# Five inversion rounds instead of six, and seven products in four more groups of an MLP

## The chip, the cores and the metric

The kernel runs on one core of one Trainium2 chip. The metric is the device time of one execution in microseconds; the median of three runs before the change is 639.98 us.

## The reference

Attention with a delta rule for 4 batches, 8 heads, 768 tokens and a head width of 48, then a Fourier mixing over tokens and features, a layer norm and an MLP 384 to 1536 to 384, all in fp32:

```python
k_n = k / (np.linalg.norm(k, axis=-1, keepdims=True) + 1e-06)
state = np.zeros((B, H, D, D), dtype=np.float32)
for t in range(S):
    kt, vt, bt = (k_n[:, :, t], v[:, :, t], beta[:, :, t, None])
    y[:, :, t] = np.einsum('bhd,bhde->bhe', q[:, :, t], state)
    v_old = np.einsum('bhde,bhd->bhe', state, kt)
    state = state + bt[:, :, :, None] * np.einsum('bhd,bhe->bhde', kt, vt - v_old)
...
x = np.ascontiguousarray(y.transpose(0, 2, 1, 3)).reshape(B, S, H * D)
mixed = np.real(np.fft.fft(np.fft.fft(x, axis=1), axis=2)).astype(np.float32)
u = x + mixed
mu = np.mean(u, axis=-1, keepdims=True)
var = np.mean((u - mu) ** 2, axis=-1, keepdims=True)
un = (u - mu) / np.sqrt(var + 1e-06)
ch = np.maximum(un @ w_ch1, 0.0) @ w_ch2
return (u + ch).astype(np.float32)
```

## The kernel before

**Units and rounds.** A unit is 128 tokens of one batch with its eight heads; there are 24 of them, `u` = 0 to 23, six to a batch (batch 1 is units 0 to 5, in the code `b = 0`). In a unit the recurrence over tokens becomes the inverse of a unit lower triangular matrix for each head, put together from blocks of 32 by 32. A round takes several units through one inversion (`begin`, `invert`): the blocks stand in one tile `rr` of 128 x 1024, 30 steps of a product (L878) and a sum (L883) on VectorE, two scale multiplies (L677, L892) and two transposes by blocks (L662, L895). The tile always has place for four units. Batch 1 goes by a way of its own in two rounds; batches 2 to 4 go in the six rounds that `SIZES` tells. After its inversion a unit's chain (`ahead`, `step`, `outputs`) carries the state on and writes its rows of `x`.

**Slots.** A unit's data (`k`, `q`, `v` and what is made of them) lie in a slot; there are six, and unit `u` takes `slots[u % GS]`. `R1` is the mixing buffer: the folds (L1257 to L1263) write it and the sequence transform (`seq6`) reads it and writes the input of the feature transform (`feat`) into it.

**Mixing and MLP.** When a batch's six units are done, `mixing(b)` folds `x` over tokens and features, does the two transforms by matmuls with tables, normalises, and gives the MLP three groups of 256 tokens. A group's MLP has six chunks of 256 hidden values. `mlp` is the plain form: `first(i)` is 6 matmuls of 256 columns into one PSUM bank, its ReLU is copied to `R0`, and `second(i)` is 4 matmuls of 384 columns, accumulated over the six chunks in two banks. `mlpw` has the second layer in seven products, 7 matmuls of 192 columns a chunk in four banks: for these VectorE makes difference tables of the weights (`tables`, L1572), four sums of the hidden values a chunk (`sums`, L1642), and combines the products at the end (L1779). In this chip's fp32 one matmul of the program is two passes of TensorE. `mlpw` is used for the last group of batch 3 and all three of batch 4.

**Order.** Every engine issues in the order of the program. `Plan.op` only lists operations; `Plan.issue` reads the string `ORDER`, which names the operation, where there is a choice its engine, and the PSUM banks it takes, and sometimes a filler matmul (L2056 to L2062, behind them no one waits). So the string sets the order on all engines.

Of the kernel before, what the change touches and what calls it, by code (L numbers as in the profile page):

```python
# [16 lines left out]
SIZES = 3, 3, 3, 3, 3, 3  # L17
# [17 lines left out]
WF = 2, 2  # L35
NW, IV, IV1, WP = 9, 7.4111, 10.4756, -12.4024
# [29 lines left out]
IeIkErCwuADGBGeCOAOAJhEsGBFNBJFJFFLJDE5CF2JHJHHFCFOHHKBEuBF5CJKJKEzFCE6BHGCGaBFRCJEFSCE2FPCDOGfBFQCJ
TJTEtCFTEJiJSJSE3CJjF3JUJUE7DrBFUCHLHE8CE9BNnE7F6GFXCGgNzFSDsBFWCE+F7CJRJRJkFVCDhDhGhF+CJlE-BJLNoNoH
NGiFeHMJNFfEBFgBF8CIuFYHFFhCGjGlCF9BFiFaCJMFbCGF4CFZBJVJOF-FFcBDDFjCGmHGCCNqNqJmFnNsNsGnCFdBJPwuAJXG
DBN-FzFkGABFoCNrE6HOFpCDxDxJWFqFmCJQGBCFrCGEGFHPJnJnIUGoCGKFlCJYGGCOCOCDgGFCGHCFOQOQGNCJZGpBHSGJoJoG
MCGqBDtCKBKBGLBEHTBJrJrwuAIWJpJpGkBGOIXJqJqHVBGrHGJCJsJsGPBHUCGICGsCGTHRCJaOPGsGQHWCNtNtGUCGVBN3N3Gv  # L70
CImGWGtCNpNpHQBGRCInKCKCGuCHXGGXBGSCNuNuG2ORORGwCHIvG4CG5BN4N4HYCG3FBJtOSOSHZBHbBOBOBGyCG6IoJvJ0J0Gz
EHGxBNwNwG7CDuBJ+J+G1CG-G0BJzJzG8HACHBBOgOgHaCJuN8N8HCDpG+CJ1J1OTCGG9BNvGZIwJ2J2HcHEOUCKsRYRYHDCKrHe
CHiOVCJwHfCEKvHkCJxHdCHjGFHlBHhCHgCKtHoOfHjKzJ9J9HmKuRvKvODHBKyHnCKwRbRbHqCHpBIfHrKAKAOECOFBJ-J-HtCH
sBRcRcK0HuRkRkK1OGECN0N0HvCK4NxNxJ3HzRXRXK7KxHwHBN6N6OJH1CRwRwK8OWDFHyCHxBK2NyNyH0BK3RjRjH2OaOZRgRgK
DK-LNAGRaRaK6OIK5H4CRsRsJ5KEK9RoRoLCOHLDKFK+RZRZLWBELARxRxH3CLBOXLGOYN7FiLEOLJyRyRyOKObLOLFRnLWLKLIR
fHsLJLHR-K5LLLXSASALMKMKMIYOhOhLPONN1N1IgOiOiOeN9N9LYJ4LUCLTCSCSCOMJ6RpRpLQBN+N+RzHDJ7LcCLZBKOKOwvGO
cLaCLbCR1BLfCGLVCSfJ8LoBFLgOdLeCKYKYLhLSCLiLxDGSBSBOOLpLjKWKWLRCR0COjCFKLKLLqLyLrN5N5LkwuAOlCKXKXLsR
2HGOkCRmRmLdBLlKGSQSQLmLtOmBFKHKJKJR6LuL0SPOILvLnL6AELwKVKVOrMYOoLzOnMVMZCOpL7MWDOtMaCMDEBKIMXCOqKjK
jOuMmCMEN2N2OwRdRdKfKfReReKKKKL1OyMbDKkKkOzO5KZL2SRSRMGRqRqKbL8O0SSSSO1R7L9R4RlRlMFL3O6KhKhO2MpBKNKN
RiRiMcBKgKgRhRhR5R8KiKiKaMgAKcMqBKdO3KPO+O-KRPAMHMfEDR3O7CKQPBShPCPDOsPEPFL4PGMnCL+MdGKlPHPIPJPKKSPL  # L80
R9PMSDBHKeMeCSTFCL-KTSECMjGSFBKnMISVCPNSUCPOKmR+PPSGBHKUSWCFSKSJPQMiPRSaMhCPSMASXSLSISOSHSYSNSbSdMBP
TMkCSeKoMlSgKpL5MCSiMzMMABPUPVMoPWMNSjPXMwMOKqPYMPM0GPZMrM1CPaPbPcPdPeSkPfMxBSlPgMsMyCPhPiMQSmM2AMJP
jMKPkPlSnMRPmSuPnM4GPoM3CSvPpPqScMuSwMSSxPrM6BAPsM5CSySpPtPuSzS0PvO4PwPxS1M9PySqS2SsCPzP0SZP1P2S3P3S
4SrCP4M7FP5P6O8CP7M+DM8CSMQZQaS5O9BNASoS6P8P9S7Q4S8P+GS9QbCP-CS+M-CQAHMLS-NBFQCCTAMTQBCTBTCTDTETFMtN
DTGNCCTHQcCQDCTIQECMUTJTKTLQFGDTMQdETNYVYVQGFCQgCTOYUTKNEHTPQICQHBQJCTQQLCQhCTRTSTTTUNGTVNFCTWQKCQ5Q
fCTXQeCTYTZTaQMCQ6GQNQiFHTbQODETcQoCYYNBNLNHQnCTdRrLuQmCNOQQCTeTfQ7BTgThQPTiQjCHNJQSFTjQlCQUGEQkCQTY
JTgQ8ATkQRCNIYfQSQpHCQ-CTlYgYgQVCNPFTmRACQqYKYKQ9BNMDRtRtTnNQCQ+BQtBToQrCRBCFTpQsCQWYLYLNNCQuRCAHYhY
hRHCTqQvGDQXCYMYMRECNRBYiYiQxCQwRuRuRFCTrRDCYXYXQYc1YjHDULZOQzCUMYlCQ1AEYkCQ0UNDTsYwYwQyCYmCHYOYOUOC
RGBQ3YvQxRIGDTtNSBUPFRLCTuEYqYoNTBTvBYNTuURCRKBUSCYnUQBStBUTCYyYyRJYtYsUqRMEYpYQYQTwGYxYxRNUUFDTxCYr
# [159 lines left out]
def kernel(  # L249
# [24 lines left out]
    GS = 6  # L274
# [1821 lines left out]
```

## Time and profile before

| | |
|---|---|
| runs | 639.98 us median of 3 (639.46 to 642.2) |
| profiled execution | 640.02 us, of which the span is 638.2 us |
| TensorE clock granted | 0.999 |
| PE matmul / weight load busy | 616.2 us (97%) / 509.8 us (80%) |
| DVE (VectorE) busy | 522.3 us (82%), 1563 instructions |
| ACT (ScalarE) busy | 268.2 us (42%) |
| POOL (GpSimd) busy | 30.4 us (5%) |
| HBM | 25.82 MB read, 4.72 MB written |

In the profile a line such as "L351 PE MATMUL pp<-w,R 128*128 128x384 f32 x384 | 133.3, 491 | 0.0" is a group: source line, engine, operation, output and inputs, the part of the array that is used, the shape, the count, then busy us, mean ns of one, and idle time ahead of them. L351 is the helper through which nearly all matmuls go. Matmuls overlap, so their spacing is read from starts. `R` is `R0` or `R1`, `w` the MLP's weights or memory beside them, `gd`, `rr`, `tmp` the inversion's tiles, `eo` and `pm` the mixing's, `us` slots.

### The profile page before, as it was taken

The page shows a single profiled execution, that of the slowest core. Times are in us where ns is not written, and L with a number is a line of the kernel's source. Part 1 is how long each engine was busy: PE and PEld are TensorE (multiplying, and loading weights), DVE is VectorE, ACT ScalarE, POOL GpSimd, SP SyncE. Part 2 cuts the span into 40 slices and gives each one's busy share as a digit, 9 for nine tenths or more (in the row PEclk, how much of TensorE's full clock was granted, in tenths as well). Part 3 has the DMA queues.
Part 4 walks back from the last instruction along what each step waited for, and adds up shares of the span by engine and source line. Part 5 has one row for each costly group of instructions (what it writes and reads, how often), then busy time and mean ns, then how long its engine had stood idle before and what let it go on. Part 6 is the DMA issues. An engine that isn't in the chain of part 4 may idle for free.

```text
span 638.2 us, 22753 instructions
## 1 busy us (share of the span) xinstructions
PE 616.2 (97%) x9694; PEld 509.8 (80%) x9694; DVE 522.3 (82%) x1563; ACT 268.2 (42%) x837; POOL 30.4 (5%) x42
## 2 busy tenths in 40 slices
PE   8988989999999999999999999999999999999997
PEld 7667889876778777877777778778778789999997
DVE  5998899899998788999876899998846868767554
ACT  6898856442454426415754323433322112322120
POOL 2022411010000000000000000000000000000000
PEclk9999999999999999999999999999999999999999
DMA  8747454400022342100231430000000000010002
GB/s 206 223 122 164 109 117 91 115 2 1 1 40 52 74 90 60 20 2 2 41 71 38 88 80 1 2 25 4 2 4 3 1 2 1 2 50 2 26 1 74
DMA packets 87171, 32.01 MB, mean 50 GB/s; under 512 B 77724, under 2 KB 82557, under 8 KB 87069
## 3 DMA queue, kind: packets, MB, share of 16 engines
q1 hardware_dynamic: 86877, 30.32, 20.1%
q8 instruction: 76, 1.25, 0.8%
q14 instruction: 26, 0.21, 0.1%
q10 hardware_dynamic: 192, 0.23, 0.1%
HBM read 25.82 MB, written 4.72 MB: 48 GB/s over the span
## 4 chain that ended last, share of the span: by engine, by line
PE 76%; DVE 11%; SPq 3%; DMA 3%; ACT 3%; issue 2%; DVEq 0%; ACTq 0%
PE pp L351 73%; SPq L402 3%; PE pp L354 2%; DMA x<-in_moe_w_ch_dram 2%; DVE R L1257 1%; ACT us L360 1%; DMA us<-in_q_dram 1%; DVE tmp L768 1%; DVE w L774 1%; DVE w L1850 1%; PE pp L2056 1%; DVE eo L1257 1%; DVE tmp L878 1%; DMA ws<-in_moe_w_ch_dram 1%; DVE rr L797 0%
## 5 line engine op out<-in xcount | busy, mean ns | idle before, releaser
L351 PE MATMUL pp<-R,w 128*128 128x256 f32 (+1 forms) x832 | 180.8, 366 | 0.0
L351 PEld LDWEIGHTS pp<-R,w 128*128 128x128 f32 x832 | 146.1, 190 | 19.2
L351 PE MATMUL pp<-w,R 128*128 128x384 f32 x384 | 133.3, 491 | 0.0
L351 PEld LDWEIGHTS pp<-w,R 128*128 128x128 f32 x384 | 70.6, 190 | 41.1 <-issue 0.3
L360 ACT ACTIVATE us<-pp 128x256 f32<-128x256 f32 (+3 forms) x205 | 67.2, 342 | 76.1 <-PE pp L351 54.2
L351 PE MATMUL pp<-us 64*64 64x64 f32 (+4 forms) x2784 | 72.8, 230 | 3.1 <-issue 1.7
L351 PEld LDWEIGHTS pp<-us 64*64 64x64 f32 (+2 forms) x2784 | 60.1, 131 | 11.8 <-issue 6.0
L878 DVE TENSOR_TENSOR tmp<-rr 128x108 f32<-128x108 f32 (+11 forms) x180 | 59.6, 336 | 2.8
L883 DVE TENSOR_TENSOR rr<-rr,tmp 128x108 f32<-128x108 f32 (+11 forms) x180 | 57.7, 326 | 2.6
L1511 ACT ACTIVATE R<-pp 128x512 f32<-128x512 f32 x37 | 21.9, 593 | 69.4 <-PE pp L351 69.4
L351 PE MATMUL pp<-u,us 64*64 64x48 f32 (+2 forms) x1472 | 44.2, 216 | 4.0 <-issue 2.1
L351 PEld LDWEIGHTS pp<-u,us 64*64 64x64 f32 (+1 forms) x1472 | 38.0, 130 | 10.5 <-issue 4.9
L1686 DVE TENSOR_TENSOR us<-us,pp 128x256 f32<-128x256 f32 x64 | 26.4, 415 | 18.4 <-ACT us L360 14.5
L360 ACT ACTIVATE us<-us,nr 128x48 f32<-128x48 f32 x120 | 28.5, 322 | 9.0 <-DVE nr L685 8.4
L360 ACT ACTIVATE R<-pp 128x384 f32<-128x384 f32 (+7 forms) x50 | 19.2, 403 | 29.8 <-PE pp L354 16.1
L351 PE MATMUL pp<-st,us 48*64 48x48 f32 (+1 forms) x1232 | 28.8, 222 | 2.1 <-issue 1.1
L351 PEld LDWEIGHTS pp<-st,us 48*64 48x64 f32 x1232 | 23.8, 134 | 8.3 <-issue 5.5
L360 ACT ACTIVATE u<-pp 64x192 f32<-64x192 f32 (+1 forms) x54 | 17.6, 325 | 28.5 <-PE pp L351 27.5
L360 ACT ACTIVATE x<-pp 64x192 f32<-64x192 f32 (+1 forms) x60 | 19.5, 324 | 20.1 <-PE pp L351 17.5
L2062 PE MATMUL pp<-pack 64*64 64x256 f32 (+1 forms) x186 | 27.6, 384 | 0.0
L351 PE MATMUL pp<-us,gd 128*128 128x192 f32 x144 | 27.5, 326 | 0.0
L351 PEld LDWEIGHTS pp<-ft,R 97*128 97x128 f32 (+1 forms) x192 | 23.8, 191 | 2.8 <-ACT R L360 0.3
(185 smaller groups left out, 994.5 us busy)
## 6 DMA issues: line engine op xcount, KB each, us to landing
out_dram<-x SPq DMA_DIRECT2D x11, 384.0 KB
x<-in_moe_w_ch_dram SPq DMA_DIRECT2D x11, 242.0 KB
R<-in_moe_w_ch_dram SPq DMA_DIRECT2D x8, 256.0 KB
us<-in_k_dram SPq DMA_DIRECT2D x36, 48.0 KB
us<-in_q_dram SPq DMA_DIRECT2D x36, 48.0 KB
us<-in_v_dram SPq DMA_DIRECT2D x36, 48.0 KB
ws<-in_moe_w_ch_dram SPq DMA_DIRECT2D x5, 242.0 KB
us<-in_k_dram SPq DMA_DIRECT2D x6, 192.0 KB
```

The source lines that it names most:

```text
L351: I(nc.tensor.matmul(o, lhsT=lhsT, rhs=rhs, start=start, stop=stop, skip_group_check=True))
L354: I(nc.tensor.matmul(o, lhsT=src, rhs=ident[p0:p0 + n, p0:p0 + n], is_transpose=True, start=start, stop=True, skip_group_check=True))
L360: I(nc.scalar.activation(o, i, ACT.Copy, **({} if scale is None else {"scale": scale})))
L402: I((nc.sync if q == "SP" else nc.scalar).dma_start(out=o[x], in_=i[x]))
L768: I(eng(e).tensor_tensor(T_, sub(j + 1, 16, j, j + 1).broadcast_to([128, 2, n, j]), sub(j, j + 1, 0, j).broadcast_to([128, 2, n, j]), op=A ...
L774: I(eng(e).tensor_tensor(w, w, T_, op=ALU.add))
L878: I(eng(e).tensor_tensor(T_, R[:, :, j + 1:32, j:j + 1].broadcast_to([128, ns, n, j]), R[:, :, j:j + 1, 0:j].broadcast_to([128, ns, n, j]) ...
L883: I(eng(e).tensor_tensor(R[:, :, j + 1:32, 0:j], R[:, :, j + 1:32, 0:j], T_, op=ALU.add))
L1257: I(eng(e).tensor_tensor(o, i0, i1, op=op))
L1511: I(nc.scalar.activation(o, s, ACT.Relu))
L1686: vec(256, lambda e: I(nc.vector.tensor_tensor(o, i0(), i1(), op=ALU.add)), [], [aH] + list(wr), pr - P.ev, use=n)
L2062: I(nc.tensor.matmul(pst[bank][x, 0:256], lhsT=w[x, 0:128 // tiles], rhs=w[x, 0:256], start=True, stop=True, skip_group_check=True))
```

## The change

Constants, with the order string replaced as a whole:

```diff
-SIZES = 3, 3, 3, 3, 3, 3
+SIZES = 4, 4, 4, 3, 3
+PLACE = (0, 1, 2, 3, 4, 5, 0, 1, 2, 3, 6, 7, 4, 5, 0, 1, 2, 3, 4, 5, 0, 1, 2, 3)
+SPARE = 10, 11
...
+BEFORE = (1, 0), (1, 1), (2, 0), (2, 1)
...
 ORDER = """
-APBABAaAbAbAZwrAAAAcAcACDAKBA-A-AIBAYAEBBABAA9A9A+A+AQDAODAGDAFDALDAdBCAJDAUDARAfCANDAeCAgEFAHDICICA
+APBAAAQDAbAbAGBANBATyMAAHBABAcAcACBAaAFBAMBA9A9ALBADBAKBA-A-AEDAZAODA+A+AYBABAAIDAJDAdBCARAgDEAeCAfB
```

Two slots more in the mixing buffer, for units 10 and 11; what reads or writes them is ordered with the rest of that buffer (`z.own`):

```diff
+    slots += [(R1, SLOT), (R1, 0)]
...
-        z.t, z.o = slots[u % GS]
+        z.extra = u in SPARE
+        z.t, z.o = slots[PLACE[u]]
+        z.key = (id(z.t), z.o) if z.extra else id(z.t)
```

The scale multiplies of `begin` and `invert` become two, of 512 and 256 columns, that leave out a part above the diagonal:

```diff
-        vec(1024, lambda e: I(nc.vector.tensor_tensor(
-            R, R, gb[:, 32:64][:, :, None].broadcast_to([128, 32, 32]), op=ALU.mult)),
-            [agb(1)], [aR], pr, port=True)
+        for x, y in ((slice(16, 32), 32), (slice(0, 16), 16)):
+            vec(16 * y, lambda e, x=x, y=y: I(nc.vector.tensor_tensor(
+                R[:, x, 0:y], R[:, x, 0:y], gb[:, 32:64][:, x, None].broadcast_to([128, 16, y]), op=ALU.mult)),
+                [agb(1)], [A(rr0, o + 32 * x.start, o + 32 * x.stop)], pr, port=True)
```

The first two groups of batches 2 and 3 (`BEFORE`) go through `mlpw`, with a plain first layer, their tables in the mixing buffer (built anew for each of the two batches behind its feature transforms), the sums in `ws`, the hidden values in `R0` in a ring of two, and three PSUM banks: product 4 is split into 128 and 64 columns in the free ends of two banks.

```diff
+        if (b, 0) in BEFORE:
+            tables(pr, True)
...
-            if (b, g) >= WF:
+            if (b, g) in BEFORE:
+                mlpw(b, g, pr)
+            elif (b, g) >= WF:
...
-        acc = [Bank("win") for _ in range(4)]
-        T = [wt(k)[0] for k in range(4)]
-        ht, ho = slots[2]
+        early = (b, g) in BEFORE
+        acc = [Bank("win") for _ in range(3 if early else 4)]
+        T = [wt(k, early)[0] for k in range(4)]
+        ht, ho = (R0, hto) if early else last[2]
+        zs = ws if early else gd0
...
+        split = {4: ((0, 384, 0, 128), (1, 384, 128, 192))} if early else {}
...
-                            mm(P_(k), *ops(i)[k], i == 0 and place[k][1] == 0, i == W6 - 1)
+                            l, r = ops(i)[k]
+                            for q, c, n0, n1 in split.get(k, ()):
+                                mm(psum(acc[q])[:, c:c + n1 - n0], l, r[:, n0:n1], False, i == W6 - 1)
+                            if k not in split:
+                                mm(P_(k), l, r, i == 0 and place[k][1] == 0, i == W6 - 1)
```

Three places in the order. First PE, the start of the MLP of batch 2's first group. `w_72` and `w_73` are the weights of the two layers, `R_81` is `R0` and `R_98` is `R1`; the number behind `pp` is a PSUM bank. Before, two chunks of the first layer and then the second layer, four rows a chunk:

```order
L351 MATMUL pp_63<-R_81,w_72 128x256 x6
L351 MATMUL pp_68<-R_81,w_72 128x256 x6
L351 MATMUL pp_65<-w_73,R_81 128x384
L351 MATMUL pp_61<-w_73,R_81 128x384
L351 MATMUL pp_65<-w_73,R_81 128x384
L351 MATMUL pp_61<-w_73,R_81 128x384
```

The same place in the changed kernel:

```order
L357 MATMUL pp_67<-R_81,w_72 128x256 x6
L357 MATMUL pp_61<-R_81,w_72 128x256 x6
L357 MATMUL pp_63<-w_73,R_81 128x192
L357 MATMUL pp_63<-R_98,ws 128x192
L357 MATMUL pp_67<-R_98,ws 128x192 x2
L357 MATMUL pp_64<-w_73,ws 128x192
L357 MATMUL pp_64<-w_73,R_81 128x192
L357 MATMUL pp_63<-R_98,R_81 128x128
L357 MATMUL pp_67<-R_98,R_81 128x64
```

A chunk of the second layer has eight matmuls instead of four, in three banks instead of two, and five of them read what DVE has made (`R_98` the tables, `ws` the sums).

Second PE, batch 2's mixing, from the end of the sequence transform (`tab`) to the feature transforms (`ft`). Before, with sixteen rows of the 64-wide kind shortened to their first two and last two by "...":

```order
L351 MATMUL pp_66<-tab,R_98 96x64
L351 MATMUL pp_66<-tab,R_98 96x2x64 x2
L351 MATMUL pp_62<-us_79 64x2x64
L351 MATMUL pp_65<-us_79 64x2x64
...
L351 MATMUL pp_62<-us_79 64x2x64
L351 MATMUL pp_65<-us_79 64x2x64
L351 MATMUL pp_68<-ft,R_98 128x97
L351 MATMUL pp_68<-ft,R_98 128x96
```

And in the changed kernel:

```order
L357 MATMUL pp_68<-tab,R_98 95x64
L357 MATMUL pp_68<-tab,R_98 95x2x64 x2
L2096 MATMUL pp_63<-pack 128x256
L357 MATMUL pp_61<-ft,R_98 128x97
L357 MATMUL pp_61<-ft,R_98 128x96
L357 MATMUL pp_66<-ft,R_98 128x97
```

The work of a unit of the next round that stood between the two transforms stands elsewhere, and one filler matmul stands in its place.

Third DVE, behind the feature transforms of batch 2, where the tables are built in the changed kernel; L888 and L893 are the two operations of an inversion step (L878 and L883 before), L1658 the sums:

```order
L1586 TENSOR_TENSOR R_98<-w_73,R_98 128x576
L888 TENSOR_TENSOR tmp<-rr 128x228
L1586 TENSOR_TENSOR R_98<-w_73 128x576
L1586 TENSOR_TENSOR R_98<-R_98,w_73 128x576
L1586 TENSOR_TENSOR R_98<-w_73 128x576
L1425 TENSOR_TENSOR eo_100<-pp_65,ss_107 128x191
L893 TENSOR_TENSOR rr<-rr,tmp 128x19x12
L1658 TENSOR_TENSOR ws<-R_81 128x128
L1658 TENSOR_TENSOR ws<-ws,R_81 128x128
L1658 TENSOR_TENSOR ws<-R_81,ws 128x128
L888 TENSOR_TENSOR tmp<-rr 128x234
L1658 TENSOR_TENSOR ws<-R_81 128x128
```

None of the L1586 and L1658 rows stands in this part of the order before; there the inversion steps, the mixing's rows (L1410 to L1421) and copies of hidden values (L1513) alternate.

243 lines of the change are left out of this document (129 added, 114 removed).

## The prediction, made before the changed kernel ran

> **What bounds the kernel now.** I read the profile's first part, then the busy time in eight stretches, then PE's waits behind the first stretch, and last PE's timeline for the time between the starts of its passes. In the second fence the columns are length, PE, PEld, DVE, ACT, POOL, PEclk, DMA share and GB/s.
>
> ```profile
> PE 616.2 (97%) x9694; PEld 509.8 (80%) x9694; DVE 522.3 (82%) x1563; ACT 268.2 (42%) x837; POOL 30.4 (5%) x42
> ```
>
> ```profile
> core 0: us, PE busy (x) PEld busy (x) DVE busy (x) ACT busy (x) POOL busy (x), PEclk, DMA share, GB/s
> 0.00:104.00 104.00, 93.70 (x2348) 79.85 (x2349) 90.78 (x297) 77.70 (x236) 23.61 (x34) 1.00 0.62 151
> 104.00:168.00 64.00, 63.77 (x508) 48.91 (x511) 60.89 (x174) 29.26 (x93) 5.61 (x6) 1.00 0.17 41
> 168.00:249.00 81.00, 77.98 (x1823) 61.33 (x1822) 69.97 (x196) 34.45 (x106) 0.56 (x2) 1.00 0.29 62
> 249.00:287.00 38.00, 37.94 (x255) 29.87 (x254) 34.89 (x107) 14.21 (x51) 0.31 (x1) 1.00 0.05 9
> 287.00:380.00 93.00, 89.55 (x1929) 70.08 (x1928) 76.33 (x216) 43.74 (x145) 0.31 (x1) 1.00 0.26 55
> 380.00:427.00 47.00, 47.00 (x297) 36.94 (x295) 44.37 (x134) 18.68 (x67) 0.00 (x0) 1.00 0.03 9
> 427.00:505.00 78.00, 76.91 (x1690) 60.12 (x1690) 57.64 (x159) 21.48 (x66) 0.00 (x0) 1.00 0.01 3
> 505.00:638.00 133.00, 129.36 (x866) 122.72 (x865) 87.44 (x287) 28.72 (x79) 0.00 (x0) 0.99 0.05 19
> ```
>
> ```profile
> PE pp L351 <- issue: 3.0, 6, 0.9
> PE pp L354 <- DMA us<-in_q_dram: 2.2, 3, 0.8
> PE pp L351 <- DVE eo L1263: 0.5, 1, 0.5
> ```
>
> From 104 us on PE is idle for 534 − 522.5 = 11.5 us in all (sum of the lower seven rows), at a granted clock of 1.00, and the waits that the profile can name there are a handful. So behind the first stretch the time is PE's work: what is taken from its passes is taken from the end, as long as no new wait comes. The second engine to watch is DVE: 95% busy in 104 to 168, 92% in 249 to 287, 94% in 380 to 427, but 74% in 427 to 505 and 66% behind that. Before 104 us, PE is "busy" for 93.7 us with waits and filler passes among it; the passes of that stretch say little about its end.
>
> **PE, the second layer.** Four groups of 256 tokens, the first two of batch 2 and of batch 3, change from plain to seven products. Each has six chunks. A plain chunk is 4 matmuls of 384 columns, and a matmul is two passes (x8 in the timeline for 4 in the program); a chunk of seven products is 7 matmuls of 192 columns.
>
> ```profile
> 148.80 5.34 PE L351 MATMUL pp<-R,w 128*128 128x256 f32 x24
> 153.98 5.32 PE L351 MATMUL pp<-w,R 128*128 128x384 f32 x16
> 159.14 5.34 PE L351 MATMUL pp<-R,w 128*128 128x256 f32 x24
> ```
>
> ```profile
> 567.76 0.49 PE L351 MATMUL pp<-w,us 128*128 128x192 f32 x2
> 568.09 1.14 PE L351 MATMUL pp<-us,gd 128*128 128x192 f32 x6
> 569.06 0.49 PE L351 MATMUL pp<-w,gd 128*128 128x192 f32 x2
> 569.39 0.49 PE L351 MATMUL pp<-w,us 128*128 128x192 f32 x2
> 569.71 0.49 PE L351 MATMUL pp<-us,us 128*128 128x192 f32 x2
> 570.04 1.26 PE L351 MATMUL pp<-R,w 128*128 128x128 f32 x8
> ```
>
> The durations overlap, so I take start to start. Sixteen passes of 384 columns: 159.14 − 153.98 = 5.16 us, 322.5 ns each, 2.58 us for a chunk of eight. Fourteen passes of 192: 570.04 − 567.76 = 2.28 us, 163 ns each. The new groups have three PSUM banks instead of four, so product 4 is split into 128 and 64 columns in two banks: 6 matmuls of 192, one of 128, one of 64. For narrow passes:
>
> ```profile
> 396.95 1.03 PE L351 MATMUL pp<-ft,R 97*128 97x97 f32 x8
> 397.82 2.78 PE L351 MATMUL pp<-R,w 128*128 128x256 f32 x12
> ```
>
> Eight passes of 97 columns take 0.87 us, 109 ns each, although the slope (322.5 − 163) / 192 = 0.83 ns a column would give about 81. So there is a floor at about 109 ns. I price 128 columns at 110 and 64 columns at the floor, 109; by the slope alone 64 columns would be 57. New chunk: 12 × 163 + 2 × 110 + 2 × 109 = 2.39 us, against 2.58: −0.19 us. Times 24 chunks: **−4.5 us**; by the slope for the narrow pass −7.0. That is the gain's lower and upper end as far as PE's passes go; I take −4.5, since the 97-column row is the nearest.
>
> A matmul here needs its own weight load each time, and the change has 8 matmuls a chunk where there were 4. The row above has fourteen passes, each with a load of its own, at 163 ns, which leaves no room for a load beside the 160 ns of the columns. [...]
>
> **PE, the order.** The changed order has ten more returns from narrow tiles to passes of the whole array. One costs about a tenth:
>
> ```profile
> 259.74 1.10 PE L351 MATMUL pp<-us 48*64 48x128 f32 x32
> 260.77 2.85 PE L351 MATMUL pp<-w,R 128*128 128x384 f32 x8
> 263.45 0.82 PE L354 MATMUL pp<-pack,pm 128*128 128x128 f32 x6
> ```
>
> Behind the 64-wide passes the chunk of eight takes 2.68 instead of 2.58. Ten of these: **+1.0 us** (0 to 2).
>
> At batch 2's mixing the cover changes. Before, narrow work of the next round stands between the sequence transform and the feature transform:
>
> ```profile
> 253.14 1.10 PE L351 MATMUL pp<-us 48*64 48x128 f32 x32
> 254.31 2.02 PE L351 MATMUL pp<-ft,R 97*128 97x97 f32 x16
> ```
>
> That is 1.17 us of cover for the copies from PSUM that the feature transform reads. Now one filler pass stands there, at most 0.4 us. And the folds ahead of it, which write the mixing buffer, have to wait for the last unit in it (units 10 and 11 lie there). I take **+1.0 us**; the lower end is 0, if the copies are done by then, the upper 3, if the folds are late as well.
>
> **DVE.** One inversion round of six goes, whose cost does not depend on how many of its four unit places are filled:
>
> ```profile
> L878 DVE TENSOR_TENSOR tmp<-rr 128x108 f32<-128x108 f32 (+11 forms) x180 | 59.6, 336 | 2.8
> L883 DVE TENSOR_TENSOR rr<-rr,tmp 128x108 f32<-128x108 f32 (+11 forms) x180 | 57.7, 326 | 2.6
> L895 DVE STREAM_TRANSPOSE gd<-rr 128x1024 f32<-128x1024 f32 x6 | 11.8, 1964 | 0.1
> L662 DVE STREAM_TRANSPOSE rr<-gd 128x1024 f32<-128x1024 f32 x6 | 11.8, 1960 | 0.1
> L892 DVE TENSOR_TENSOR rr<-rr,gb 128x1024 f32<-128x1024 f32 x6 | 7.3, 1224 | 0.2
> L677 DVE TENSOR_TENSOR rr<-rr,gb 128x1024 f32<-128x1024 f32 x6 | 7.3, 1217 | 0.1
> ```
>
> (59.6 + 57.7 + 11.8 + 11.8 + 7.3 + 7.3) / 6 = −25.9 us. The scale multiplies lose a quarter of their columns and gain an instruction: about −1. What comes:
>
> ```profile
> L1642 DVE TENSOR_TENSOR gd<-us 128x128 f32<-128x128 f32 x48 | 13.3, 285 | 4.6 <-ACT us L1718 3.1 <-ACT us L1695 1.3
> L1572 DVE TENSOR_TENSOR us<-w 128x576 f32<-128x576 f32 x4 | 3.0, 750 | 0.1
> L1779 DVE TENSOR_TENSOR x<-x,pp 128x192 f32<-128x192 f32 x20 | 6.6, 347 | 4.0 <-ACT u L360 2.3 <-PE pp L351 1.8
> L1545 DVE TENSOR_TENSOR x<-x,pp 128x384 f32<-128x384 f32 x16 | 8.7, 547 | 0.4 <-PE pp L351 0.3
> ```
>
> Four sums for each of 24 chunks, 96 × 0.285 = +27.4. Two more sets of difference tables, 16 × 0.75 = +12. 44 more combining additions × 0.35 = +15, less 8 × 0.55 of the plain groups, −4.4. Against that the order gives 29 evictions to ACT that were DVE's, by the last two rows 0.35 to 0.55 each: −13. Sum +10: DVE goes from 522 to about 532 us. ACT, at 42%, takes its 13 without anyone behind it. DVE's sum lies beside PE, and I cost it at nothing on the path, since 427 to 505 and what follows have over 60 us of room, and the round that goes leaves from the full stretches. The cover is PE's own passes; where DVE is late, each chunk waits (first rival). The other way, slots for eight units let loads start earlier: at most the 2.2 us of waits for in_q_dram above and part of the 11.5. I take **−1.5 us** for both (−6 to 0). SP issues as many loads and stores as before; those of units 10 and 11 wait for the feature transform of batch 1, and PE has two chunks and more of other work there. The first stretch is re-ordered too, at 0 ± 2: of its steps none has a new cost.
>
> **Sum.** The profiled execution took 640.02 us (span 638.2, 1.8 around it), 0.04 above the median of 639.98. 640.0 − 4.5 + 1.0 + 1.0 − 1.5 = **636.0 us**, −0.6%. The three runs before spread over 639.46 to 642.2; I count within 0.5% (636.8 to 643.2) as what this kernel's measurement can't tell from no change.
>
> **Rivals.**
> *DVE holds the chunks up; slower.* A chunk's second layer can start when its hidden values are copied and four sums, 4 × 0.285 = 1.1 us, are done. The order puts inversion steps between them (0.33 each by the two rows above), and only a first layer of 5.18 / 2 = 2.6 us lies between. With two steps waited out on top, each chunk waits 2 × 0.33 = 0.67: 16 us in 24 chunks, 8 if only batch 2's twelve suffer. 644 to 652, 648 in the middle. It decides from 0.19 us a chunk on, where the gain is gone. For it: DVE at 92 to 95% in three stretches, and the tables come right ahead of the first sums, 4 × 0.75 = 3 us at once. Against it: the same sums stand beside passes at 163 ns at 567 us. 0.18.
> *The gain is eaten; the same.* Batch 2's mixing waits its 3 us, three PSUM banks held through a group cost another 1 to 2 in the attention beside it, and nothing comes from DVE: 640.0 − 4.5 + 1.0 + 4.5 = 641. 0.16.
> *More than the arithmetic; faster.* The narrow pass costs its slope (−2.5 more), and the idle 11.5 us halve as loads are earlier and a round's chain of 30 steps is gone: 640.0 − 7 + 1 + 1 − 4 = 631. 0.17.
> *The weight loads don't hide; slower.* Eight more passes a chunk at the floor of 109 ns would be 0.87 us, less the 0.19: 24 × 0.68 = +16, 656. [...] 0.03.
> *The first stretch's new order costs 3 or more.* About 641 to 645. 0.03.
>
> **How the numbers follow.** The forecast, 633.5 to 638.5, has 0.43. Two thirds of it lie below 636.8, 0.29, and with the 0.17 that makes faster 0.46. Its other third, 0.14, the eaten gain and 0.01 of the first stretch's case: same 0.31. Slower is DVE, the weight loads and the rest of the first stretch: 0.18 + 0.03 + 0.02 = 0.23. The range takes the forecast, the faster case with its end at 629, the eaten gain, and half of the DVE rival up to 647.
>
> **What would show it.** Right: a chunk of a new group takes 2.4 us, with some 109 ns for a 64-column pass; PE's idle time behind the first stretch stays near 10 us; the two inversion steps count 150 each instead of 180 and DVE's busy time comes to about 532 us. Wrong: PE waits for the 128-column sums in the groups of batch 2 (DVE rival), a gap ahead of the feature transform of batch 2 over 2 us, narrow passes near 60 ns, or a first stretch whose end moves by more than 2 us.

## The result and the profile after

| | before | changed |
|---|---|---|
| median | 640.54 us of 20 runs (637.25 to 645.44) | 637.21 us of 20 (631.75 to 646.57) |
| ratio | | 0.9925, 95% interval 0.9898 to 0.9952 |
| profiled execution | 640.02 us, span 638.2, clock 0.999 | 638.45 us, span 636.4, clock 0.993 |

The kernel is faster by 3.3 us, 0.75%. One run of the changed kernel, at 646.57 us, lies over 1.5% above its fastest and is left out of comparisons. The page's first part and its clock row:

```profile
PE 612.9 (96%) x9890; PEld 534.6 (84%) x9890; DVE 523.2 (82%) x1618; ACT 282.3 (44%) x890; POOL 29.8 (5%) x33
PEclk9999998999999999999999999999989999999999
```

PE's busy time is 3.3 us down with 196 passes more. DVE's has hardly moved (522.3 before), and two slices of the clock row are below 9. The same eight stretches of the program as before, at their new places (length, PE, PEld, DVE, ACT, POOL, PEclk, DMA share, GB/s):

```profile
0.00:104.00 104.00, 94.41 (x2386) 80.88 (x2386) 91.45 (x291) 79.24 (x250) 23.70 (x27) 1.00 0.63 153
104.00:168.00 64.00, 61.21 (x478) 47.20 (x479) 57.18 (x172) 28.71 (x89) 5.45 (x4) 0.97 0.30 70
168.00:258.00 90.00, 89.42 (x2043) 70.21 (x2042) 77.96 (x219) 41.27 (x136) 0.31 (x1) 1.00 0.17 34
258.00:290.00 32.00, 31.71 (x354) 29.45 (x354) 30.08 (x96) 14.27 (x45) 0.00 (x0) 1.00 0.06 17
290.00:383.00 93.00, 91.70 (x1803) 80.57 (x1802) 75.04 (x236) 40.19 (x130) 0.32 (x1) 1.00 0.26 53
383.00:430.00 47.00, 46.90 (x341) 39.76 (x340) 45.72 (x147) 23.79 (x84) 0.00 (x0) 1.00 0.01 1
430.00:533.00 103.00, 99.05 (x1797) 90.28 (x1796) 76.01 (x225) 29.23 (x88) 0.00 (x0) 0.98 0.04 14
533.00:637.00 104.00, 98.52 (x700) 96.27 (x698) 69.78 (x239) 25.65 (x73) 0.00 (x0) 0.99 0.04 16
```

Before, the clock was 1.00 in all but the last of its rows. Now it is 0.97 in 104 to 168 and 0.98 in 430 to 533. One microsecond at a time, the second place looks so:

```profile
463.00:464.00 1.00, 1.00 (x7) 1.00 (x6) 0.85 (x3) 0.00 (x0) 0.00 (x0) 0.87 0.00 0
464.00:465.00 1.00, 1.00 (x5) 1.00 (x5) 0.48 (x2) 0.00 (x0) 0.00 (x0) 0.50 0.09 16
465.00:466.00 1.00, 1.00 (x5) 1.00 (x5) 0.00 (x0) 0.00 (x0) 0.00 (x0) 0.50 0.00 0
466.00:467.00 1.00, 1.00 (x6) 1.00 (x4) 0.00 (x0) 0.00 (x0) 0.00 (x0) 0.50 0.00 0
467.00:468.00 1.00, 1.00 (x62) 0.83 (x65) 0.14 (x1) 0.00 (x0) 0.00 (x0) 0.93 0.00 0
```

PE counts as busy there, but at half the clock: 0.13 + 3 × 0.50 + 0.07 = 1.7 us lost. The clock record has it as one stretch of 3.41 us, and another of 3.41 us at 105.3. Both stand behind gaps in PE's work, which its timeline shows, with a third behind which nothing happened:

```profile
104.58 0.69 PE L357 MATMUL pp<-ft,R 95*128 95x97 f32 x4 [0.94 <-DVE R L368]
140.12 0.68 PE L360 MATMUL pp<-pack,R 64*128 64x64 f32 x15 [1.93 <-ACT w L1861]
462.74 0.29 PE L357 MATMUL pp<-u,us 64*48 64x48 f32 x5 [1.85 <-issue]
```

One of the new chunks in PE's timeline, with the transpose behind it:

```profile
296.20 0.49 PE L357 MATMUL pp<-w,R 128*128 128x192 f32 x2
296.52 1.14 PE L357 MATMUL pp<-R,ws 128*128 128x192 f32 x6
297.50 0.49 PE L357 MATMUL pp<-w,ws 128*128 128x192 f32 x2
297.82 0.49 PE L357 MATMUL pp<-w,R 128*128 128x192 f32 x2
298.15 0.55 PE L357 MATMUL pp<-R,R 128*128 128x128 f32 x4
298.54 0.50 PE L360 MATMUL pp<-pack,pm 128*128 128x128 f32 x3
```

The twelve passes of 192 columns take 298.15 − 296.20 = 1.95 us, 162.5 ns each; the four of the split product 0.39. That is 2.34 us a chunk, 0.24 less than the plain 2.58. In 24 chunks PE saves 5.8 us where they stand. Against the span of before: 638.2 − 5.8 + 3.4 (two half-clock stretches) + 1.9 (the gap ahead of 462.74) = 637.7; the measured span is 636.4, so all the rest of the change gave 1.3.

### The profile page after: what moved, and what is told of

Same layout as the page of the kernel before. It is cut to its first block, busy times and chain, and to the rows that moved or that the text cites. A ratio compares the mean times of both kernels' runs of the same rounds, so it can differ in the third digit from the quotient of the medians.

```text
span 636.4 us, 23238 instructions
## 1 busy us (share of the span) xinstructions
PE 612.9 (96%) x9890; PEld 534.6 (84%) x9890; DVE 523.2 (82%) x1618; ACT 282.3 (44%) x890; POOL 29.8 (5%) x33
## 4 chain that ended last, share of the span: by engine, by line
PE 77%; DVE 7%; SPq 6%; ACT 5%; issue 3%; DMA 2%; DVEq 0%; ACTq 0%
PE pp L357 73%; SPq L408 6%; PE pp L360 3%; ACT us L366 2%; DMA us<-in_q_dram 1%; DVE gd L620 1%; PE pp L2090 1%; DVE rr L718 1%; DMA R<-in_moe_w_ch_dram 1%; ACT w L1861 1%; PE pp L2096 1%; ACT pb L366 1%; DVE w L1880 0%; ACT u L366 0%; DMA x<-in_moe_w_ch_dram 0%
## 5 line engine op out<-in xcount | busy, mean ns | idle before, releaser
L357 PE MATMUL pp<-w,R 128*128 128x384 f32 (+1 forms) x288 | 92.0, 443 | 0.0
L357 PEld LDWEIGHTS pp<-w,R 128*128 128x128 f32 x288 | 51.8, 191 | 21.8 <-issue 0.8
L357 PE MATMUL pp<-us 64*64 64x64 f32 (+4 forms) x2560 | 64.2, 233 | 1.2 <-issue 0.7
L357 PEld LDWEIGHTS pp<-us 64*64 64x64 f32 (+2 forms) x2560 | 54.7, 133 | 5.5 <-issue 2.1
L888 DVE TENSOR_TENSOR tmp<-rr 128x240 f32<-128x240 f32 (+12 forms) x150 | 48.8, 329 | 1.7
L893 DVE TENSOR_TENSOR rr<-rr,tmp 128x168 f32<-128x168 f32 (+11 forms) x150 | 48.0, 325 | 2.0
L357 PE MATMUL pp<-u,us 64*48 64x48 f32 (+2 forms) x1360 | 39.8, 216 | 3.8 <-issue 3.0
L366 ACT ACTIVATE R<-pp 128x384 f32<-128x384 f32 (+10 forms) x63 | 23.9, 404 | 34.0 <-PE pp L360 14.7
L366 ACT ACTIVATE u<-pp 64x192 f32<-64x192 f32 (+1 forms) x66 | 21.4, 325 | 19.3 <-PE pp L357 17.9
L357 PE MATMUL pp<-R,ws 128*128 128x192 f32 x144 | 28.4, 332 | 0.1
```

The source lines that it names most:

```text
L357: I(nc.tensor.matmul(o, lhsT=lhsT, rhs=rhs, start=start, stop=stop, skip_group_check=True))
L366: I(nc.scalar.activation(o, i, ACT.Copy, **({} if scale is None else {"scale": scale})))
L888: I(eng(e).tensor_tensor(T_, R[:, :, j + 1:32, j:j + 1].broadcast_to([128, ns, n, j]), R[:, :, j:j + 1, 0:j].broadcast_to([128, ns, n, j]) ...
L893: I(eng(e).tensor_tensor(R[:, :, j + 1:32, 0:j], R[:, :, j + 1:32, 0:j], T_, op=ALU.add))
```

## The experiments

Theory A, the prediction's: the passes carry the gain, DVE's work is covered. Theory B: DVE's work (sums, tables, inversion) holds PE up, and the round that goes is what counts. Theory C came out of the profile after: what the short passes save is given back by gaps and by the clock behind them. Ratios are to the kernel before in the same series; the interval is in brackets. Each run also has its mean granted clock, so span × (1 − clock) is an estimate of what the run lost to the clock, good to some 0.3 us since the clock has three decimals, and too high where PE was not what held the kernel up, as in the last microseconds of a run (in the profile above the clock is 0.50 from 634.4 us on, behind PE's last work). "Without the lost clock" means below that this is taken off each run, and the mean is given with its standard error.

| run | median us (range, runs) | ratio |
|---|---|---|
| again, no edit | 638.21 (634.12 to 641.26, 12) | 0.9945 [0.9916, 0.9974] |
| beside, no edit | 635.48 (633.42 to 641.51, 12) | 0.9946 [0.9919, 0.9972] |
| plain_second | 637.71 (633.47 to 642.38, 12) | 0.9949 [0.9915, 0.9982] |
| small_sums | 635.3 (632.13 to 638.3, 8) | 0.9913 [0.9879, 0.9948] |
| round_back | 659.44 (656.93 to 660.79, 6) | 1.0285 [1.0245, 1.0324] |
| before_short | 641.4 (638.71 to 645.41, 12) | 0.9999 [0.9970, 1.0029] |
| after_short | 637.51 (633.36 to 641.81, 12) | 0.9933 [0.9902, 0.9963] |
| loads_first | 638.32 (632.32 to 641.66, 12) | 0.9953 [0.9925, 0.9982] |
| wide_fill | 638.89 (634.07 to 643.83, 12) | 0.9952 [0.9923, 0.9981] |
| rounds_only | 636.78 (633.61 to 642.57, 12) | 0.9968 [0.9938, 0.9999] |
| seven_b2 | 635.02 (633.33 to 638.71, 12) | 0.9943 [0.9918, 0.9967] |
| seven_b3 | 637.78 (633.29 to 641.29, 12) | 0.9967 [0.9937, 0.9998] |

**again** is the changed kernel without an edit, beside the next ones.

> The changed kernel itself, unedited. Theory A (the work on PE fell by more than forecast, and part of it is lost again where PE idles for 1 us or more, after which its granted clock is half for 3.41 us at a time): the place and the number of half-clock stretches differ from execution to execution, and the time goes with the mean clock: about 632 to 633 us at 1.00, 634 at 0.995, 640 at 0.99. Theory B (the spread is something else, DMA or the queue of loads): times between 632 and 641 with no tie to the clock.

The ratio, 0.9945, agrees with the first one. The tie to the clock is there, but looser than expected: runs at 0.991 to 0.993 lie from 634.1 to 639.2 us, where the expectation leaves 636 to 639. Its "1 us or more" is the author's estimate: half clock followed a gap of 0.94 us and not the one of 1.93.

**plain_second** makes the 24 chunks' second layers 8 passes of 384 columns again; all that DVE does for the seven products stays.

```diff
+                    if early:
...
+                        for i in chunks:
+                            h0 = sets[i][0]
+                            for a, tt in todo:
+                                mm(psum(acc[tt])[:, 0:DM], ht[:, h0 + 256 * a + 128 * tt:h0 + 256 * a + 128 * tt + 128],
+                                   w2v[:, i + W6 * a, :], i == 0 and a == 0, i == W6 - 1 and a == 1)
+                        return
```

> The second layer of the four groups is made of eight passes of 384 columns a chunk again, with order, banks, sums, tables and combining additions as in the changed kernel (the additions then combine the wrong products, and the output of these groups is not the reference's). Theory A (PE's passes carry the gain): 24 chunks x 0.24 us = 5.8 us slower than the changed kernel, about 643. Rival (the round that went from VectorE carries it): within 1.5 us of the changed kernel, about 637.

637.71 beside 638.21: the 5.8 us of the passes do not show in the median at all. Theory A's main term does not hold as it was meant, that what PE saves comes off the end. But the clocks differ, with medians of 0.997 here and 0.991 in again. Without the lost clock plain_second takes 635.2 ± 0.7 us and again 631.0 ± 0.5: by this estimate 4.2 us of the passes' 5.8 are there, and the clock takes them back. In this run's profile the longest gap of PE between 440 and 510 us is 0.58, and there is one half-clock stretch in place of two.

**small_sums** cuts the sums of the new groups to two columns.

```diff
+                n = 2 if early else 128
-                    s(j), i0, i1, op=op)), [aH] + rd, [aS(j)], pr - P.ev)
+                    s(j)[:, 0:n], i0[:, 0:n], i1[:, 0:n], op=op)), [aH] + rd, [aS(j)], pr - P.ev)
```

> The four sums of a chunk in the four groups are made for 2 columns instead of 128 (the rest of what the products read is not made, so these groups' output is wrong). It takes some 20 us from VectorE in the places where the second layers stand, and the wait for the sums with it. Theory A: no wait for them is named in the trace, so the time stays within 1.5 us of the changed kernel. Rival (VectorE holds the chunks up): faster by 3 us or more, under 634.

2.9 us less than without the edit, with intervals that overlap. Read by places it is not the sums' waits: from batch 2's sequence transform to batch 3's this run took 124.5 us against 124.8 and 125.6 of the two unedited runs then at hand, and from batch 3's to batch 4's 150.0 like both. What it gained lies ahead of batch 2, where the edit changes nothing, and without the lost clock it takes 631.3 ± 0.8 beside 631.0 ± 0.5. So no chunk waits for its sums to speak of.

**round_back** gives DVE back the round's time: 14 of the 30 products of each round twice.

```diff
+                if 9 <= j <= 22:
+                    I(eng(e).tensor_tensor(T_, R[:, :, j + 1:32, j:j + 1].broadcast_to([128, ns, n, j]),
+                                           R[:, :, j:j + 1, 0:j].broadcast_to([128, ns, n, j]),
+                                           op=ALU.mult))
```

> In each of the five rounds 14 of the 30 products of the inversion are computed twice: 70 more instructions at about 0.37 us, 26 us more on VectorE, as much as the round that was taken away, on the same chain. Theory A (VectorE has cover): slower by 2 to 6 us, since the inversions also run in the stretches where VectorE is over 90% busy. Rival (taking a round from VectorE is what brought the gain): slower by 8 us or more, above 645.

```profile
PE 621.0 (94%) x9890; PEld 538.1 (82%) x9890; DVE 549.3 (84%) x1688; ACT 282.6 (43%) x890; POOL 30.3 (5%) x33
```

DVE has 26 us more, and the kernel takes 21 more, well over the 2 to 6 expected by theory A. So DVE's work is not free: with this order, more of it goes to the end almost in full. Part of the 21 is the clock behind new waits: half-clock stretches cost 10.2 us in this profile and 3.4 in that of the changed kernel. **before_short** and **after_short** ask the other side, with less of it: 8 and 10 of the 30 steps cut to one element, in the kernel before and in the changed one (so the inverse is not complete).

```diff
+                if 12 <= j <= 19:
+                    I(eng(e).tensor_tensor(T_[:, :, 0:1, 0:1], R[:, :, j + 1:j + 2, j:j + 1], R[:, :, j:j + 1, 0:1], op=ALU.mult))
+                    return
```

> The kernel before, with 8 of the 30 steps of each of its six inversions cut to one element (both operations of the step; the inverses are wrong): about 16 x 0.26 us = 4.2 us less in each round, 25 us less on VectorE in all, as much as one round. Theory A (PE's passes carry the gain, the rounds have cover): at most 2 us faster, 638 to 640. Theory C (the inversions are what PE's leftover waits hang on, and taking a round away carries the gain): 4 us or more faster, under 636.

> The changed kernel with 10 of the 30 steps of each of its five inversions cut to one element: about 5.2 us less in each round, 26 us less on VectorE. Adding as much cost 21 us. If the inversions lie on the path in the changed kernel, taking as much away gives 10 us or more, under 628; if they are just covered, 0 to 4 us, 633 to 637.

The first part of the page of before_short:

```profile
PE 615.4 (96%) x9694; PEld 509.4 (80%) x9694; DVE 500.2 (78%) x1563; ACT 268.0 (42%) x837; POOL 30.5 (5%) x42
```

22 us less of DVE's time give nothing before (0.9999), and as much less nothing after (637.51 beside 637 to 638; without the lost clock 632.2 ± 0.5, where the three series of the changed kernel have 631.0 to 632.6). The round that goes is not, by DVE's time alone, where the gain comes from: theory B falls. DVE's work fits the order as it stands, and what is put on top does not.

**loads_first** and **wide_fill** go for the two gaps of 1.9 us. The first moves three `v` loads of two units on SP behind the last `k` load of unit 11, whose transposes stand behind the gap at 138 us:

```diff
-L408 DMA R_98<-in_v_dram 64x4x48
 L408 DMA x_97<-in_moe_w_ch_dram 121x512
...
+L408 DMA R_98<-in_k_dram 64x4x48
+L408 DMA R_98<-in_v_dram 64x4x48 x2
```

> The changed kernel with three loads of v (units 10 and 12, wanted much later) moved in the order behind the last load of k of unit 11, which is issued three places earlier by that. In the trace PE sits idle for 1.9 us at 136 to 138 us, in front of unit 11's transposes. Theory: it waits for that load, whose issue stands last in SyncE's queue at 0.62 us a piece; the idle time shrinks by 1.2 to 1.9 us, and the time by as much, about 635 to 636, a little more where half-clock stretches follow the gap. Rival (it waits for something else, the weights' copy on ScalarE that the trace names): the gap stays at 1.9 and the time at 637.

638.32: no gain. The gap went to the next unit's transposes. SP issues a `k` load at 139.88, and that they wait for it is likely, but the profile names no wait:

```profile
143.81 0.68 PE L360 MATMUL pp<-pack,us 64*128 64x64 f32 x15 [2.08 <-issue]
```

SP's queue as a whole is late there, at up to 0.6 us an issue; one load's turn does not help. ACT, which the row of the changed kernel names, is not the cause: in the profiles of plain_second and wide_fill the gap ahead of the same transposes is put down to the load itself (DMA R<-in_k_dram). wide_fill puts five filler matmuls of 256 columns ahead of the place of the second gap, so that PE's instructions would be used up more slowly:

```diff
 L357 MATMUL pp_64<-u_84,us_80 64x48
+L2096 MATMUL pp_61<-pack 128x256 x5
 L357 MATMUL pp_61<-u_84,us_80 48x48 x8
```

> The changed kernel with five filler matmuls of the whole array (256 columns, 0.43 us each, 2.1 us of PE in all) put into a stretch of narrow tiles of units 19 to 22, some 3 us ahead of the place at 461 us where PE stands idle for 1.9 us within one unit's matmuls and waits for nothing that the profile shows. Theory (instructions run out: narrow tiles take some 90 instructions a us and the next 16 KB of instructions come too late): the gap goes, and with it the half-clock stretch behind it, the time stays within 1 us of the changed kernel or falls by 1 to 2 us. Rival (a wait that the profile does not name): the gap stays and the time grows by 2 us.

```profile
469.34 0.56 PE L357 MATMUL pp<-u,us 64*48 64x48 f32 x16 [1.49 <-issue]
```

The gap went down to 1.49 us and 6 us on, with no half-clock stretch behind it in this profile, and the fillers cost what that saved.

The last four are one series on one chip. **rounds_only** has none of the four groups in seven products (no sums, no tables, plain additions), all else as changed; **seven_b2** has them in batch 2's two groups alone, **seven_b3** in batch 3's alone. All three still do the whole computation.

```diff
+SEVEN = ((1, 0), (1, 1))
...
+        plain = early and (b, g) not in SEVEN
...
+                    if plain:
...
+                        for i in chunks:
+                            for a, tt in todo:
+                                h0 = sets[i][0] + 256 * tt + 128 * a
+                                mm(psum(acc[tt])[:, 0:DM], ht[:, h0:h0 + 128], w2v[:, i + W6 * a, :],
+                                   i == 0 and a == 0, i == W6 - 1)
+                        return
```

> The changed order of everything else, but all four groups of batches 2 and 3 go through the plain second layer again: 24 chunks of 8 passes of 384 columns, no 128-column sums, no difference tables, two plain additions a group in place of eleven. DVE has 96 sums, 16 tables and 36 additions less, some 50 us of work. Theory 1 (DVE's work in the changed kernel is covered, and the gap and the half-clock stretch near 461 us come with the narrow passes): the same time as the earlier run with the 24 chunks plain and the sums kept, 637.7, at most 1.5 beside it, and no gap of over 1.5 us near 461. Theory 2 (the sums and tables hold PE up in small waits everywhere): 50 us less of DVE's work gives 3 us or more, 634 or less. Theory 3 (all of the gain is the passes of the seven products): 643, by 24 x 0.24 above the unedited kernel's 637 to 638.

> The seven products stay in the two groups of batch 2; the two groups of batch 3 are plain again, without sums, tables and the nine extra additions of each. Theory 1 (each chunk of seven products gives its 0.24 us; in batch 3 the short passes bring a gap of 1.9 us for PE's instructions near 461 us and a half-clock stretch of 1.7 behind it, which cost more than the 12 chunks give): 637.7 - 12 x 0.24 = 634.8 us, with no gap over 1.5 us near 461; some 2.5 to 3 below the unedited kernel of the same call. Rival (what the chunks save is waited for again later, wherever they stand): the same as the unedited kernel, 637.5 to 638.5.

> The other half: the seven products stay in the two groups of batch 3 and batch 2 is plain again, without sums, tables and extra additions. Theory 1: 12 x 0.24 = 2.9 us lost in batch 2, the gap near 461 us and the half-clock stretch behind it stay: 638.2 + 2.9 = 641 by the unedited kernel, or 637.7 - 2.9 + 3.6 = 638.4 by the run with all chunks plain; I expect 638.4 to 641, slower than the kernel with batch 2's alone by 3.5 or more. Rival (saved time is waited for again later, or DVE's relief in the full stretches of batch 2 counts): 637.5 or less.

> The changed kernel without an edit, beside the three others on one chip: 637.2 to 638.2, as in the two series so far.

The medians, 636.8, 635.0, 637.8 and 635.5, have intervals of 2 us to each side, so they only lean: batch 2's chunks give some 2 us, batch 3's none. Without the lost clock the four take 633.9 ± 0.4, 631.8 ± 0.6, 633.0 ± 0.4 and 631.3 ± 0.3, and the kernel before in the same series 638.8 ± 0.3: batch 2's chunks give about 2, batch 3's under 1, and the new rounds and order, without any of the products, 4.9. The profiles tell more, since each stretch stands apart. First from batch 2's sequence transform to batch 3's, in seven_b2, beside, rounds_only and seven_b3 in turn:

```profile
250.49:375.11 124.62, 122.95 (x2154) 109.70 (x2153) 104.65 (x328) 55.56 (x176) 0.31 (x1) 1.00 0.21 44
```

```profile
251.06:376.03 124.97, 123.04 (x2153) 109.78 (x2152) 104.61 (x328) 55.35 (x176) 0.31 (x1) 1.00 0.21 44
```

```profile
258.71:385.47 126.76, 125.42 (x2058) 98.06 (x2057) 86.42 (x255) 54.72 (x174) 0.31 (x1) 1.00 0.20 43
```

```profile
256.38:383.38 127.00, 125.43 (x2058) 98.06 (x2058) 86.36 (x254) 54.69 (x174) 0.31 (x1) 1.00 0.20 43
```

With the seven products 124.62 and 124.97, without them 126.76 and 127.00: 12 chunks give 2.1 us of their 2.9, although DVE has 18 us more to do there. The two other unedited profiles have 124.84 and 125.62, and plain_second, plain here too, 127.47. Then from batch 3's sequence transform to batch 4's, in seven_b2 and rounds_only (plain in this stretch), and beside, seven_b3 and the first profile of the changed kernel (seven products):

```profile
375.11:523.75 148.64, 147.06 (x2039) 116.83 (x2038) 107.22 (x307) 51.64 (x167) 0.00 (x0) 1.00 0.03 10
```

```profile
385.47:533.05 147.58, 146.51 (x2039) 116.61 (x2038) 107.19 (x307) 51.65 (x167) 0.00 (x0) 1.00 0.03 10
```

```profile
376.03:524.14 148.11, 144.30 (x2135) 128.43 (x2134) 123.78 (x378) 52.32 (x169) 0.00 (x0) 1.00 0.02 7
```

```profile
383.38:530.70 147.32, 144.58 (x2136) 128.44 (x2134) 123.94 (x378) 52.32 (x169) 0.00 (x0) 1.00 0.02 8
```

```profile
378.96:528.95 149.99, 145.93 (x2135) 130.03 (x2134) 123.76 (x378) 52.25 (x169) 0.00 (x0) 0.99 0.02 7
```

148.64 and 147.58 plain; 148.11 and 147.32 in seven products, and 149.99 where the half-clock stretch came too. The two pairs overlap, so between a gain and a loss of 1 us nothing can be told here. PE is busy 2.2 to 2.5 us less (146.8 in the middle to 144.30 and 144.58) and idle for most of that more: in beside a gap of 2.13 us stands at 458, in seven_b3 one of 1.36 at 461; in seven_b2 and rounds_only no gap there is over 0.6. So theory C fits batch 3, and the rival, that saved time is waited for wherever it stands, fails for batch 2. The expected sizes were too clear-cut: rounds_only came within 1 us of the 637.7 of theory 1, seven_b2 at 635.0 for 634.8, seven_b3 at 637.8 just under its 638.4 to 641; but seven_b2 was to lie 2.5 to 3 below beside and lies 0.5 below, and beside itself, at 635.5, came 1.7 below the least expected of it. In the medians of that series batch 3's chunks did beside no measurable harm, and no version shown here is measurably faster than the changed kernel.

## Why the prediction was right, and where it was not

The forecast was 636.0 with 633.5 to 638.5 as the likeliest case; 637.21 lies in it, and faster had the largest chance. Its sum, though, came out by misses that cancel, so that the number is luck in good part.

**The passes, −4.5.** In place they gave 5.8. The term was undersized by the narrow pass: at the floor of 109 ns the four split passes would take 0.44 us, and they take 0.39, which with 110 for each of the wide ones leaves 85 for a narrow one. Resolved in the trace, the two narrow passes start 58 and 112 ns ahead of what follows them (where that is of the whole array), so the slope's 57 was right for one of them and the other waits for the next pass. What fails is the step behind it, "what is taken from its passes is taken from the end, as long as no new wait comes": 2.1 of 2.9 us came off batch 2's stretch, about none in batch 3, where a new wait came, and what was left the clock mostly took back.

**The weight loads.** Eight more a chunk cost nothing beside the wide passes: the 162.5 ns of a 192-column pass are the 163 of before. Only behind the second narrow pass the next one comes 112 ns on instead of 58 in the ten chunks that work of the whole array follows, and 205 in the others, which narrow tiles follow; whether its weight load is the reason no run shows, and 24 × 0.054 = 1.3 us, an estimate from the 112 and the 58, would be its whole price. The rival's 0.68 us more a chunk no run shows; a chunk takes 2.34 us.

**The order, +1.0 and +1.0.** Ahead of batch 2's feature transform stands no gap; it starts 0.43 us behind the one filler:

```profile
257.83 1.32 PE L357 MATMUL pp<-tab,R 128*96 128x64 f32 x11
258.99 0.60 PE L2096 MATMUL pp<-pack 128*128 128x256 f32 x2
259.42 1.80 PE L357 MATMUL pp<-ft,R 97*128 97x97 f32 x14
```

So that +1.0 was at most 0.4. The returns from narrow tiles to the whole array were not told apart from other small waits.

**DVE, nothing on the path.** Right for what it is, by both short runs, although six of a chunk's eight matmuls (not five, as the section on the change has it) read what DVE has made. The rival by which chunks wait for their sums would need 8 us or more; small_sums and the 124.6 to 125.0 us of batch 2 leave no room for it, and PE's waits behind 104 us name no sum:

```profile
PE pp L357 <- issue: 3.3, 3, 1.9
PE pp L360 <- ACT w L1861: 1.9, 1, 1.9
PE pp L357 <- DVE R L368: 1.2, 2, 0.9
PE pp L360 <- DVE tmp L888: 0.7, 1, 0.7
```

The 532 us of busy time did not come: it is 523.2. The two step groups count 150 as they should, and adding up the lengths of all DVE records gives 610.5 us before and 621.0 after, about the predicted +10. But busy time counts overlapping records once, and neighbours overlap:

```profile
290.94 0.29 DVE L1658 TENSOR_TENSOR ws<-R 128x128 f32<-128x128 f32 x1
291.15 0.35 DVE L1422 TENSOR_TENSOR eo<-pp,ss 128x193 f32<-128x193 f32 x1
291.42 0.26 DVE L888 TENSOR_TENSOR tmp<-rr 128x108 f32<-128x108 f32 x1
```

The sum at 290.94 is 0.29 long, and the next instruction starts 0.21 behind its start. The error of the step is that it took mean lengths for occupied time; 148 such instructions of the seven products took 522.5 − 488.8 = 33.7 us (beside less rounds_only), where their lengths add up to 49. DVE's work was covered, so this cost the forecast nothing.

**The room won, −1.5, and the first stretch, 0 ± 2.** Behind 104 us PE is idle for 533 − 518.5 = 14.5 us, not some 10: the two gaps of 1.9 are new. On the other side all four groups plain, with the new rounds and order, are at 0.9968 [0.9938, 0.9999] of the kernel before. By this comparison rounds and order give about 2 of the 3.4 us that beside has, where the prediction had +0.5 for them; without the lost clock they give 4.9. This is the sum's largest miss. Part of it is ahead of batch 2, but two executions of the same kernel differ there by more than the size asked for: without the time lost to the clock, the span is 633.0 in the first profile and 628.2 in beside, and nearly all of these 5 us arise before batch 2's sequence transform. A landmark tells more, and by it one of the prediction's own signs of being wrong came. Batch 1's feature transform begins at 103.8 and 104.7 us in the two profiles of the old order and at 96.9 to 101.9, 99.5 in the mean, in the twelve of the new one, with 20 more PE passes begun ahead of it and 7 to 11 fewer DVE instructions. From there to the end, without half-clock time, the old order takes 533.5 and 533.0 us, the changed kernel 531.5, 533.4 and 530.2 (first profile, again, beside) and rounds_only 532.9. So most of the gain lies in the first stretch, which the sum had at 0 ± 2, and only some 0 to 3 us behind it, where the passes are. What in the new order of the first stretch gives it no run tests.

**What was not in the sum.** The clock. It was read as 1.00 behind 104 us and taken as given. Half-clock stretches cost 3.4 us in the changed kernel's profile, 3.4 in again, 3.4 in beside, 8.5 in rounds_only, 1.7 in seven_b2, from 1.7 to 10.2 in all twelve profiles of the new order, and nothing in the two of before and before_short (the last 5 us of each profile, where PE runs out of work, left aside). In 19 runs of the first series of the changed kernel the ten with a mean clock of 0.995 or more have a median of 634.1, the nine below 639.3. Without the 3.4 us the time would have been near 634, and the forecast 2 us too high: the miss on the clock made up for the misses on the rounds, the order and the first stretch.

## What to carry to other kernels

Where PE is full, price a change of its passes with what has to feed them: here the same operations in more and shorter passes came with a new gap of 1.85 us, and the clock behind it cost 1.7 us more, so look for the new gaps first and read the clock in windows of one microsecond. Occupied time of an engine comes from starts or from the busy column, not from count times mean length (33.7 us against 49 for the 148 DVE instructions here). When a median moves less than the spread, compare profiles from landmark to landmark: a stretch that agreed to 0.8 us between profiles of one kernel told 2.1 us apart which the medians could not. Set each run's clock beside its time as well: two kernels with nearly equal medians differed by 4 us once the lost clock was taken off.

## What the runs showed of the hardware

**Half clock after short gaps.** In the changed kernel's profile PE's clock went to 0.50 for 3.41 us twice: at 105.33 us behind a gap of 0.94 us, and at 463.73 behind one of 1.85. It stayed at 1.00 behind the gap of 1.93 us that ends at 140.12 (from 136 to 160 us) and behind one of 1.10 that ends at 491.23, behind one of 1.36 in seven_b3 (1.00 from 383.38 to 530.70) and behind one of 1.49 in wide_fill (1.00 from 466 to 472). In the changed kernel's profile stretches begin on a grid: 105.33 and 463.73 are 358.40 us apart, 105.0 times 3.413, and the third, at 634.40, where PE has no work left, is 170.67 us behind the second, 50.0 times. By these gaps size does not decide: 0.94 was followed by half clock, 1.93 was not. The gap of 1.85 us lies within one step of that grid (460.32 to 463.73), in which PE was busy for 46%, and half clock followed; the one of 1.93 lies across two (136.05 to 139.47 to 142.88), busy for 63% and 81%, and none followed. From 120 us to 627 that is the only step with PE busy for under 60%, and the only one that half clock follows. Ahead of 120 us this does not separate them: the step ahead of 105.33 has PE busy for 72%, and one of 56% (57.55 to 60.96) was followed by none (1.00 from 40 to 100). In seven_b3 the clock is 0.50 from 102.0 us at the latest, and its gap of 0.94 us ends only at 102.55. What decides there stays open.

In rounds_only the gap at the same place, ahead of batch 1's feature transform, is 0.93 us, and half clock follows for some 13.7 us, 0.8 + 4 + 4 + 4 + 0.9 in these rows, four times 3.413:

```profile
102.00:106.00 4.00, 3.07 (x27) 2.55 (x28) 3.96 (x8) 4.00 (x11) 1.66 (x2) 0.90 0.19 37
106.00:110.00 4.00, 4.00 (x68) 3.42 (x63) 3.29 (x13) 1.75 (x8) 0.00 (x0) 0.50 0.06 12
110.00:114.00 4.00, 4.00 (x20) 3.83 (x19) 2.02 (x7) 1.41 (x8) 0.00 (x0) 0.50 0.00 0
114.00:118.00 4.00, 4.00 (x18) 3.73 (x17) 4.00 (x8) 1.30 (x3) 1.45 (x1) 0.50 0.27 56
118.00:122.00 4.00, 4.00 (x18) 3.46 (x17) 2.87 (x6) 0.58 (x2) 0.00 (x0) 0.89 0.44 100
```

**Gaps of PE behind blocks of the instruction queue.** The gap near 461 us is put down to "issue". One instruction queue moves 77 blocks of 16 KB in the changed kernel's profile. One block's transfer began at 459.95 and landed at 461.23, and PE, which had started 451 passes and weight loads since the block before began to come (455.89), stood from 460.89 to 462.74, to 1.51 us behind the landing. The gap of 1.10 us that ends at 491.23, put down to "issue" too, ends 1.30 us behind the landing of a block (489.93), and in the kernel before one of 0.90 that ends at 458.16 ends 1.50 behind one (456.66). With batch 3 in seven products the gap near 461 is 1.85 us in the changed kernel's profile and 1.36 in seven_b3, and with five wide fillers 1.49 and 6 us later; in seven_b2, rounds_only and plain_second, whose batch 3 has the wide passes, PE shows none of over 0.6 us there. That the supply of instructions is its cause agrees with all of this; no run changed the supply itself, so it is not shown directly.
